# Moving forty matmuls behind the first output-projection rounds of every segment

## The chip, the cores and the metric

The kernel runs on one core of one Trainium2 chip. The metric is the device time of one launch in microseconds. Three runs of the kernel before took 1028.8, 1029.67 and 1029.64 us; their median is 1029.64 us.

## The reference

The input x has 2048 tokens of width 640. It is layer-normalised and goes through a recurrent attention of 64 segments of 32 tokens. Each segment attends to 8 memory rows and its own 32 tokens (causally), in 32 heads of width 128. The 8 output rows that belong to the memory are the memory of the next segment, so the segments form one serial chain. After that come a residual sum, a second layer norm, and a feed-forward block with a squared ReLU.

```python
for s in range(n_seg):                                   # 64 segments
    h = jnp.concatenate([mem, xs], axis=1)               # 8 memory rows + 32 tokens
    q = jnp.einsum('btd,dhe->bhte', h, Wq)               # k and v alike
    scores = jnp.where(mask, jnp.einsum('bhqe,bhke->bhqk', q, k) * scale, -1e9)
    o = jnp.einsum('bhqk,bhke->bhqe', _softmax(scores), v)
    o = jnp.einsum('bhte,hed->btd', o, Wo)
    mem = o[:, :M, :].copy()                             # feeds the next segment
    outs.append(o[:, M:, :])
# then h = x + attention, and h + (relu(norm(h) @ w1 + b1)**2) @ w2 + b2
```

## The kernel before, in words

All weights are held in SBUF as bf16, and the whole order of the work is written out by hand: each engine gets its instructions in the order of the Python text, and waits for others through semaphores.

`step(b, sp)` is one segment. Only the 8 memory rows depend on the segment before, and so the step takes them, with 24 of the tokens, through the projections; the last 8 tokens of four segments at a time ("tails") are projected ahead, as filler work (`fill`) in the later part of a step. `project` computes q and k in two halves each, with the small operand as the weights (`proj`, L206, 20 matmuls of 128x512 for a half, four column groups of TensorE at a time). Values go the same way: `ps0` is the even heads' half (20 matmuls), copied to `v[:, 0:512]` by ScalarE (L502), and `ps1` the odd heads' half, copied to `v[:, 512:1024]` (L523). "Even" and "odd" here are the heads whose index in the head group is in the first or second half of v; the code calls them n = 0 and n = 1.

Around the change TensorE's order in a step is this:

- two q and k projections with the scores of the memory rows of n = 0 between them;
- the first 8 matmuls of `ps0`, the token scores of n = 0 (`token_scores(0)`), the last 12 of `ps0`, the first 8 of `ps1`;
- the memory scores of n = 1 (`scores(1)`, L416 and L421, 20 matmuls), the token scores of n = 1 (L493, 16);
- `token_values` for the segment before (L355, 32 matmuls; L360, 8): probabilities of the previous step's tokens times the previous step's v, into columns 0 to 255 of the four banks of the PSUM tile `po`;
- `values(0)`: the memory rows' values of n = 0 (L449, 16 matmuls; L454, 4), into columns 256 to 287 of the same banks. They read `v[:, 0:512]` and the probabilities `pT0`, which VectorE has transposed (L440). VectorE copies the result to `oT` (L213, in `evac`);
- the last 12 matmuls of `ps1`;
- `wo_rounds(main, pw, 0, 6)`: 24 matmuls of the output projection (L238), whose weights are `oT`, n = 0;
- `values(1)` (L449, L454), which read `v[:, 512:1024]`; ScalarE copies their result (L215);
- `wo_rounds` 6 to 8 (8 matmuls), some filler, `wo_rounds` 8 to 16 (32), which need n = 1 of `oT`.

Then ScalarE and VectorE add the two halves of the output projection (`wo_out`, L245 and L246), ScalarE copies the token values out of `po` (`token_out`, L365), and `mem_to_hT` (L316, L318) puts the new memory rows in front of the next step's tokens. `po` has one buffer. Its first matmul into each bank of a step carries `start=True`, which opens the bank; all others add or write into what is opened.

Step 0 has no token values of a segment before; step 63 (`last`) has no memory values. After the steps the token values of segment 63 are made once more outside of `step` (L800), and then the feed-forward block runs in four tiles of 512 tokens.

Of the kernel before, what the change touches and what calls it, by code (L numbers as in the profile page):

```python
# [16 lines left out]
def kernel(  # L17
# [19 lines left out]
    M = A_mem0.shape[1]  # L37
# [8 lines left out]
    NS = S // SEG  # L46
# [48 lines left out]
    for g in range(G):  # L95
        r = slice(32 * g, 32 * g + 32)
# [15 lines left out]
    def head(p):  # L112

        n, g, j = p // 16, p // 4 % 4, p % 4
        return g * HG + j * 2 + n
# [115 lines left out]
    def wo_rounds(lhs, pw, h0, h1):  # L231

        for h in range(h0, h1):
            for kh in range(2):
                for ch in range(2):
                    j = kh * 2 + ch
                    p = h // 8 * 16 + kh * 8 + h % 8
                    nc.tensor.matmul(pw[32 * j:32 * j + 32, 0:DH], lhsT=lhs(p), rhs=wov2[:, head(p), ch],  # L238
                                     start=(h == 0), stop=(h == 15))
# [105 lines left out]
    oTg = oT[:].rearrange("p (n g j) q -> p n g j q", n=2, g=G)  # L345
    back = []

    def token_values(s, v, vt4, po):

        sp = s % 4  # L350
        pTk, pTx = back.pop()
        for i in range(HG):
            for g in range(G):
                r = slice(32 * g, 32 * g + 32)
                nc.tensor.matmul(po[:, g, i * 32:(i + 1) * 32], lhsT=v[r, i * E:(i + 1) * E], rhs=pTk[r, i, :],  # L355
                                 start=(i == 0), stop=False, skip_group_check=True)
        for u in range(2):
            for g in range(G):
                r = slice(32 * g, 32 * g + 32)
                nc.tensor.matmul(po[:, g, u * 128:(u + 1) * 128].rearrange("p (j q) -> p j q", q=32)[:, :, HD:32],  # L360
                                 lhsT=vt4[r, sp, u, :], rhs=pTx[r, u], start=False, stop=True, skip_group_check=True)

    def token_out(s, po):
        for n in range(2):
            nc.scalar.copy(out=oTg[:, n, :, :, M:NK],  # L365
                           in_=po[:, :, n * 128:(n + 1) * 128].rearrange("p g (j q) -> p g j q", q=32))
        nc.gpsimd.tensor_copy(out=oTts[s // 4 % 2][:, :, s % 4 * TL:(s % 4 + 1) * TL], in_=oT[:, :, 32:NK])
# [10 lines left out]
    prev = {}  # L378

    def step(b, sp, v=None):  # L380
        s = b * 4 + sp
        last = s == NS - 1
# [3 lines left out]
        if not ready:  # L386
            v = s2.tile([128, EG], BF16, tag="v", name="v")
# [55 lines left out]
        def values(n, pT, po):  # L443
            c0 = 256 + n * 4 * M
            for j in range(4):
                i = n * 4 + j
                for g in range(G):
                    r = slice(32 * g, 32 * g + 32)
                    nc.tensor.matmul(po[:, g, c0 + j * M:c0 + (j + 1) * M], lhsT=v[r, i * E:(i + 1) * E],  # L449
                                     rhs=pT[r, j * M:(j + 1) * M], start=(s == 0 and i == 0), stop=False,  # L450
                                     skip_group_check=True)
            for g in range(G):
                r = slice(32 * g, 32 * g + 32)
                nc.tensor.matmul(po[:, g, c0:c0 + 4 * M], lhsT=vt4[r, sp, n, :], rhs=pT[r, 32:64],  # L454
                                 start=False, stop=True, skip_group_check=True)

        def values_out(n, po):
            c0 = 256 + n * 4 * M
            evac(n == 0, oTg[:, n, :, :, 0:M], po[:, :, c0:c0 + 4 * M].rearrange("p g (j m) -> p g j m", m=M))
# [19 lines left out]
        vt4 = vt4s[b]  # L479
# [33 lines left out]
        if ready:  # L513
            run(fill, DC)
        po = pop.tile([128, G, 512], F32, tag="po", name="po")
        if s:
            token_values(s - 1, prev["v"], prev["vt4"], po)
        if not last:
            values(0, pT0, po)
            values_out(0, po)  # L520
# [10 lines left out]
        pw = chn.tile([128, 512], F32, tag="ch", name="pw")  # L531
        main = lambda p: oT[:, p, 0:32]
        wo_rounds(main, pw, 0, 6)
        if not last:
            values(1, pT1, po)
            values_out(1, po)
# [197 lines left out]
    for b in range(NB):  # L734
        for sp in range(4):
# [47 lines left out]
            if 2 <= e <= NK4 + 1:  # L783
                late.append(lambda e=e: prep_stats0(e - 2))
                mid.append(lambda e=e: prep_norm0(e - 2))
            step(b, sp, v0 if b + sp == 0 else None)

    def end_output(s):
# [8 lines left out]

    end_output(NS - 2)
    po = pop.tile([128, G, 512], F32, tag="po", name="po")
    token_values(NS - 1, prev["v"], prev["vt4"], po)  # L800
    token_out(NS - 1, po)
    for k in range(NK4):
        prep_bias(0, k, ht0[k][:])
# [3 lines left out]
    for t in range(S // NT):  # L807
# [6 lines left out]
        for fc in range(FC):  # L814
            ps = mmtile()
            for c in range(DC):
                if fc < FFULL:
                    nc.tensor.matmul(ps[:], lhsT=w1[:, c, fc * 128:(fc + 1) * 128], rhs=hnT[:, c, :],  # L818
                                     start=(c == 0), stop=(c == DC - 1))
                    continue  # L820
                for hh in range(2):
                    nc.tensor.matmul(ps[FREM * hh:FREM * (hh + 1), 0:HT], lhsT=w1[:, c, fc * 128:F],
                                     rhs=hnT[:, c, HT * hh:HT * (hh + 1)], start=(c == 0), stop=(c == DC - 1))
            w = NT if fc < FFULL else HT
            r = rs_[fc % 4]
# [14 lines left out]
        for q in range(NK4):  # L840
# [6 lines left out]
            for hh in range(2):  # L847
                k = pr + 2 * hh
                for fc in range(FFULL):
                    nc.tensor.matmul(y[:, hh, 0:DH], lhsT=f1T[:, fc, k * 128:(k + 1) * 128], rhs=w2[:, fc, cs],  # L850
                                     start=(fc == 0), stop=False, skip_group_check=True)
# [3 lines left out]
            for hh in range(2):  # L855
                r = slice(FREM * hh, FREM * (hh + 1))
                nc.tensor.matmul(y[:, hh, 0:DH], lhsT=f1T[r, FFULL, pr * 128:(pr + 1) * 128], rhs=w2[r, FFULL, cs],
                                 start=False, stop=True, skip_group_check=True)
# [40 lines left out]
```

## Time and profile before

| | |
|---|---|
| median of three runs | 1029.64 us |
| profiled execution, first to last instruction | 1025.5 us |
| what lies around it, to the median | 4.1 us |
| TensorE busy | 971.4 us, 95% |
| VectorE, ScalarE, GpSimd busy | 619.0, 533.2, 309.1 us |
| share of TensorE in the chain that ended last | 87% |
| granted TensorE clock, mean | 0.997 |
| first memory values to last token values | 53.5 to 890.1 us |
| token values, L355 and L360 | x2048 at 171 ns, x512 at 183 ns (median of one) |
| memory values, L449 and L454 | x2016 at 169 ns, x504 at 171 ns (median of one) |

The durations of single matmuls overlap: four or more run at a time in different parts of the array. What a group of matmuls costs is read from the starts: from the first start of a group to the first start of the next. In the step at 514 us, 32 token-value matmuls take 0.22 us in this way, though one is listed at 171 ns. "issue" in the answers is idle time for whose end the profile shows no other engine's work.

### The profile page before, as it was taken

What the parts mean: (1) busy time and instruction counts of PE and PEld (TensorE: products, weight loads), DVE (VectorE), ACT (ScalarE), POOL (GpSimd) and SP (SyncE); (2) the same over time, 40 slices, a digit from 0 to 9 for tenths busy, and PEclk for the clock granted to TensorE, in tenths of its full rate; (3) what the DMA queues carried; (4) which work ended last, traced back from release to release, by engine and by line L of the source; (5) the groups of instructions that cost most, each with busy time, mean ns of one, the idle gap of its engine ahead of it and who ended that gap; (6) DMA issues with size and microseconds to landing.
All of it is one profiled execution on the core that took longest, in us unless ns stands there. A gap on an engine that the chain in (4) does not pass through costs nothing.

```text
span 1025.5 us, 58960 instructions
## 1 busy us (share of the span) xinstructions
PE 971.4 (95%) x26951; PEld 576.6 (56%) x26960; DVE 619.0 (60%) x1740; ACT 533.2 (52%) x1229; POOL 309.1 (30%) x803
## 2 busy tenths in 40 slices
PE   5789999999999999999999999999999999999998
PEld 2345555655655555555655665555566565555565
DVE  2246666766666757666666666666666676466432
ACT  3335554555555555555555555555555555533431
POOL 1123333333333333333333332323232333443210
PEclk9989999999999999999999999999999999999999
DMA  9950101000101010001000000000000110612200
GB/s 367 397 180 21 23 7 30 7 25 6 35 7 31 6 40 8 26 11 31 11 25 11 26 16 20 17 15 27 14 22 8 47 34 7 204 55 65 77 26 26
DMA packets 39112, 51.57 MB, mean 50 GB/s; under 512 B 5968, under 2 KB 35024, under 8 KB 36944
## 3 DMA queue, kind: packets, MB, share of 16 engines
q1 hardware_dynamic: 38080, 47.48, 13.9%
q8 instruction: 210, 3.44, 1.4%
q10 hardware_dynamic: 784, 0.34, 0.1%
q14 instruction: 38, 0.31, 0.1%
HBM read 38.37 MB, written 9.44 MB: 47 GB/s over the span
## 4 chain that ended last, share of the span: by engine, by line
PE 87%; DMA 6%; DVE 2%; issue 2%; ACT 1%; SPq 1%; ACTq 0%; DVEq 0%; POOL 0%; POOLq 0%
PE ps L206 48%; PE pw L238 15%; PE y L850 5%; PE ps L818 4%; PE ps L238 3%; PE po L449 2%; PE po L355 2%; PE sm L421 2%; DMA wq<-in_B_w_dram 1%; DMA vt_d<-row 1%; PE ps L493 1%; DMA wv<-in_A_Wv_dram 1%; DMA wo<-in_A_Wo_dram 1%; PE pm L316 1%; DMA vt<-vt_d 1%
## 5 line engine op out<-in xcount | busy, mean ns | idle before, releaser
L206 PEld LDWEIGHTS <-hT 128*32 128x32 bf16 x7680 | 195.4, 97 | 179.6 <-issue 17.9
L238 PE MATMUL pw<-wo,oT 128*32 128x320 bf16 x4224 | 185.6, 300 | 7.6 <-issue 5.6
L206 PE MATMUL ps<-wv,hT 128*32 128x512 bf16 x2520 | 171.5, 379 | 2.3 <-issue 1.6
L206 PE MATMUL ps<-wq,hT 128*32 128x512 bf16 x2520 | 160.0, 382 | 5.3 <-DVE hT L318 5.3
L206 PE MATMUL ps<-wk,hT 128*32 128x512 bf16 x2520 | 159.3, 381 | 0.1
L238 PEld LDWEIGHTS <-oT 128*32 128x32 bf16 x4224 | 106.7, 96 | 59.8 <-issue 13.0
L222 ACT ACTIVATE row<-ps 128x512 bf16<-128x512 f32 x156 | 93.3, 599 | 75.5 <-PE ps L206 75.5
L227 DVE STREAM_TRANSPOSE qT<-row 128x512 bf16<-128x512 bf16 x128 | 90.3, 705 | 66.0 <-ACT row L222 65.9
L548 POOL TENSOR_TENSOR pkt<-ek,rk 128x64 bf16<-128x64 bf16 x64 | 18.8, 294 | 360.6 <-DVE rk L546 360.6
L224 ACT CAST row<-ps 128x512 bf16<-128x512 f32 x115 | 67.9, 591 | 33.1 <-PE ps L206 31.4
L325 POOL COPY kT<-kTt 128x1024 bf16<-128x1024 bf16 (+1 forms) x65 | 71.8, 1105 | 11.7 <-DVE kTt L227 11.7
L374 POOL COPY qz<-qT 128x96 bf16<-128x96 bf16 x126 | 33.4, 265 | 139.1 <-DVE qT L227 138.9
L206 PEld LDWEIGHTS <-hTt 128*32 128x32 bf16 x1920 | 53.6, 97 | 31.5 <-issue 1.3
L245 ACT COPY otmp<-pw 64x320 f32<-64x320 f32 x66 | 27.9, 422 | 81.3 <-PE pw L238 81.3
L365 ACT CAST oT<-po 128x512 bf16<-128x512 f32 x128 | 68.7, 589 | 1.6
L246 DVE TENSOR_TENSOR o<-pw,otmp 64x320 bf16<-64x320 f32 x66 | 31.8, 482 | 61.3 <-ACT otmp L245 61.3
L523 ACT CAST v<-ps 128x512 bf16<-128x512 f32 x63 | 36.9, 585 | 59.0 <-PE ps L206 59.0
L227 DVE STREAM_TRANSPOSE kT<-row 128x512 bf16<-128x512 bf16 x65 | 46.1, 709 | 31.1 <-ACT row L224 31.1
L544 DVE TENSOR_REDUCE zk<-ek 128x8 f32<-128x320 bf16 x64 | 31.1, 486 | 51.1 <-ACT ek L542 51.1
L850 PE MATMUL y<-wq,wk 128*128 128x320 bf16 x416 | 61.2, 299 | 0.4 <-DVE wk L827 0.4
L405 ACT CAST row<-ps 128x256 bf16<-128x256 f32 x126 | 40.7, 375 | 30.5 <-PE ps L206 29.9
L502 ACT CAST v<-ps 128x512 bf16<-128x512 f32 x63 | 36.9, 585 | 30.5 <-PE ps L206 30.5
(113 smaller groups left out, 1629.5 us busy)
## 6 DMA issues: line engine op xcount, KB each, us to landing
wv<-in_A_Wv_dram SPq DMA_DIRECT2D x5, 1024.0 KB
wq<-in_A_Wq_dram SPq DMA_DIRECT2D x5, 1024.0 KB
wk<-in_A_Wk_dram SPq DMA_DIRECT2D x5, 1024.0 KB
vt<-vt_d SPq DMA_DIRECT2D x60, 64.0 KB
xt<-in_A_x_dram SPq DMA_DIRECT2D x20, 160.0 KB
vt_d<-row SPq DMA_DIRECT2D x22, 128.0 KB
wo<-in_A_Wo_dram SPq DMA_DIRECT2D x2, 1280.0 KB
wo<-in_A_Wo_dram SPq DMA_DIRECT2D x4, 640.0 KB
```

What stands on the lines that cost most here:

```text
L206: nc.tensor.matmul(ps[32 * k:32 * k + 32, :], lhsT=lhs(c), rhs=wr[:, c, n, k], start=(c == 0), stop=(c == DC - 1))
L222: nc.scalar.mul(out=row, in_=ps, mul=scale)
L224: nc.scalar.copy(out=row, in_=ps)
L227: nc.vector.transpose(out=dst[:, n * 16:(n + 1) * 16, 0:32], in_=row.rearrange("p (h e) -> p h e", e=32))
L238: nc.tensor.matmul(pw[32 * j:32 * j + 32, 0:DH], lhsT=lhs(p), rhs=wov2[:, head(p), ch], start=(h == 0), stop=(h == 15))
L325: nc.gpsimd.tensor_copy(out=kT[:, h0:h1, SEG:2 * SEG].rearrange("p h (j k) -> p h j k", k=TL), in_=k.unsqueeze(2).to_broadcast([128, h1 - ...
L365: nc.scalar.copy(out=oTg[:, n, :, :, M:NK], in_=po[:, :, n * 128:(n + 1) * 128].rearrange("p g (j q) -> p g j q", q=32))
L405: nc.scalar.copy(out=row[:, u * 256:(u + 1) * 256], in_=ps[:, u * 256:(u + 1) * 256])
L502: nc.scalar.copy(out=v[:, 0:512], in_=ps0[:])
L523: nc.scalar.copy(out=v[:, 512:1024], in_=ps1[:])
L818: nc.tensor.matmul(ps[:], lhsT=w1[:, c, fc * 128:(fc + 1) * 128], rhs=hnT[:, c, :], start=(c == 0), stop=(c == DC - 1))
L850: nc.tensor.matmul(y[:, hh, 0:DH], lhsT=f1T[:, fc, k * 128:(k + 1) * 128], rhs=w2[:, fc, cs], start=(fc == 0), stop=False, skip_group_chec ...
```

## The change

The call of `token_values` for the segment before moves: from ahead of `values(0)` to behind the first 24 output-projection matmuls, ahead of `values(1)`. Which matmul opens the banks changes with it: `values(0)` does in every step that has memory values, and `token_values` only in the last step and in the call after the steps. Nothing else is edited.

```diff
-    def token_values(s, v, vt4, po):
+    def token_values(s, v, vt4, po, opens):
...
                 nc.tensor.matmul(po[:, g, i * 32:(i + 1) * 32], lhsT=v[r, i * E:(i + 1) * E], rhs=pTk[r, i, :],
-                                 start=(i == 0), stop=False, skip_group_check=True)
+                                 start=(opens and i == 0), stop=False, skip_group_check=True)
...
-                                     rhs=pT[r, j * M:(j + 1) * M], start=(s == 0 and i == 0), stop=False,
+                                     rhs=pT[r, j * M:(j + 1) * M], start=(i == 0), stop=False,
...
         po = pop.tile([128, G, 512], F32, tag="po", name="po")
-        if s:
-            token_values(s - 1, prev["v"], prev["vt4"], po)
         if not last:
             values(0, pT0, po)
             values_out(0, po)
...
         wo_rounds(main, pw, 0, 6)
+        if s:
+            token_values(s - 1, prev["v"], prev["vt4"], po, last)
         if not last:
             values(1, pT1, po)
             values_out(1, po)
...
-    token_values(NS - 1, prev["v"], prev["vt4"], po)
+    token_values(NS - 1, prev["v"], prev["vt4"], po, True)
```

## The prediction

> **What bounds the kernel now.** I read the page first, then TensorE's waits, then single steps in the timeline.
>
> ```profile
> span 1025.5 us, 58960 instructions
> ...
> PE 971.4 (95%) x26951; PEld 576.6 (56%) x26960; DVE 619.0 (60%) x1740; ACT 533.2 (52%) x1229; POOL 309.1 (30%) x803
> ...
> q8 instruction: 210, 3.44, 1.4%
> ...
> PE 87%; DMA 6%; DVE 2%; issue 2%; ACT 1%; SPq 1%; ACTq 0%; DVEq 0%; POOL 0%; POOLq 0%
> ```
>
> TensorE is the chain, so a change counts by what it does to TensorE's idle time. Queue 8 brings instructions: 210 packets, 3.44 MB, 16 KB each. TensorE has 53,911 records, so a packet holds 256 instructions, or 128 matmuls with their weight loads: call it a block.
>
> ```profile
> PE pw L238 <- issue: 5.6, 14, 1.2
> ...
> PE po L449 <- issue: 4.4, 10, 0.7
> ...
> PE po L454 <- issue: 1.8, 4, 0.6
> ...
> PE ps L206 <- issue: 1.6, 4, 0.6
> ```
>
> This is TensorE idle with nobody to wait for, 13 us in 32 places. One of them, in the step at 252 us:
>
> ```profile
> 252.65 0.37 PE L355 MATMUL po<-pTk,v 32*128 32x32 bf16 x32
> ...
> 252.93 0.17 PE L449 MATMUL po<-pTm,v 32*128 32x8 bf16 x1
> ...
> 253.81 0.26 PE L449 MATMUL po<-pTm,v 32*128 32x8 bf16 x15 [0.70 <-issue]
> ```
>
> The second memory-value matmul comes 0.88 us after the first, in the middle of a group that runs at 7 ns a matmul elsewhere. I numbered all matmuls in program order and compared each one's distance from its predecessor with the median of the same place in other steps. 55 of those up to 890 us are late, **27.6 us together**, and all of them have a number that leaves 93 on division by 128. They are block edges; 53 lie at the places below, the other two (2.2 us) outside of steps 1 to 62. After a late edge the next packet begins 1.13 us later (median; 1.05 to 1.29 for most), a packet takes 1.07 us on average, and TensorE goes on 1.41 us after its end: **3.6 us from asking to having**. A block that is run in less makes TensorE wait. [...]
>
> An undisturbed step:
>
> ```profile
> 514.16 0.58 ACT L502 CAST v<-ps 128x512 bf16<-128x512 f32 x1 [0.48 <-PE ps L206]
> ...
> 514.74 0.37 PE L355 MATMUL po<-pTk,v 32*128 32x32 bf16 x32
> ...
> 515.03 0.30 PE L449 MATMUL po<-pTm,v 32*128 32x8 bf16 x16
> ...
> 515.29 0.83 PE L206 MATMUL ps<-wv,hT 128*32 128x512 bf16 x12
> ...
> 515.95 0.99 PE L238 MATMUL pw<-wo,oT 128*32 128x320 bf16 x24
> 516.15 0.24 DVE L440 STREAM_TRANSPOSE pTm<-pmem 128x64 bf16<-128x64 bf16 x1
> 516.18 0.58 ACT L523 CAST v<-ps 128x512 bf16<-128x512 f32 x1 [0.75 <-PE ps L206]
> ...
> 516.87 0.17 PEld L449 LDWEIGHTS <-v 32*128 32x128 bf16 x16 [0.27 <-ACT v L523]
> ```
>
> By starts: token values 0.284 us (medians of 62 steps here and below), memory values 0.268, end of `ps1` 0.658, 24 output-projection matmuls 0.921. The copy of even values (L502) ends as the token values start: these now cover it.
>
> **The change part by part.** Counted in matmuls from the first token value of before, the four groups stand at 0-39, 40-59, 60-71 and 72-95; after, memory values at 0-19, `ps1` at 20-31, output projection at 32-55, token values at 56-95. The matmuls are as many, so every block edge keeps its number.
>
> *Term 1, the wait for even values.* `values(0)` now follows the token scores at once and must wait for L502, which ends 7 ns after its new place (5 to 7 in 61 of the 62 steps 1 to 62). From a ScalarE copy's end to the matmul that waits for it takes 50 to 52 ns where TensorE was idle (L502 to L206 at 868.84 us). So 57 to 59 ns a step; 62 x 0.058 = **+3.6 us**. The upper bound is the only longer distance from copy to matmul here, 111 ns from L523 to the second memory values: 62 x 0.118 = 7.3 us. I take the lower, because 111 is no wait: the start after the last output-projection matmul is 232 ns there, as at L180 with nothing to wait for. `pT0` (L440) is done 0.23 us before, 0.07 in the worst step. Behind the waiting weight load stand 20 memory values, `ps1` and 24 output-projection matmuls; L213 and L523 wait for those, and both come 0.23 us earlier than now, since the token values no longer stand ahead. `oT` reaches the output projection 0.12 us early in either order.
>
> *Term 2, odd values.* `values(1)` gets 0.284 us more cover after L523, but it doesn't wait now (232 ns as above): 0. The token values need what the last step left, long done. Changes between kinds of groups are as many as before. Step 63 and the call after the steps have no memory values and get no new wait. ScalarE's and GpSimd's steps after the output projection keep their distance to it, and no DMA moves: 0.
>
> *Term 3, edges at 32 to 95.* The block's predecessor edge lies 128 matmuls earlier, ahead of the moved groups, so the packet comes when it came; TensorE now reaches the edge later, because slow groups (`ps1`, output projection) stand ahead of it in place of the quick token values. Later by 0.97 us at 40, 1.49 at 56, 1.39 at 60, 1.00 at 71, 0.59 at 80 and 0.06 at 96 (sums of the groups above). 26 of the 55 waits lie here, 14.8 us. Less the shift of its own place each, 0.5 us is left: **-14.3 us**.
>
> *Term 4, edges at 96 to 127.* 15 waits, 6.0 us; each edge is reached 0.058 us later, packet as before: **-0.9 us**.
>
> *Term 5, edges at 128 to 159.* Their predecessors lie at 0 to 31. 37 edges, 12 waits, 4.6 us. [...] Lowest: only the 0.058 us shift counts, -0.6. Highest: all 37 wait 0.3 us more, +11. I take 0.25 us, the middle of 0.2 and 0.3, at the 12 that wait, **+3.0**, and nothing for the 25 that are on time, whose slack the trace does not tell; this is the term that I know least.
>
> Sum: 3.6 - 14.3 - 0.9 + 3.0 = -8.6. On the profiled execution 1025.5 becomes 1016.9; the 4.1 us around it stay: **1021.0 us**.
>
> [...]
>
> **The rivals.**
>
> *Slower: the waits move, they don't go.* A block edge's wait that is avoided could return at the next edge, because TensorE arrives there sooner after the request. For it: an edge at 56 was passed at 0.42 us plus its wait of some 0.6, now at 1.90, so the way to the next is up to 1.4 us shorter. Against: the next edge, at 160 to 223, lies in filler and projections at 54 ns a matmul, and no edge there waits in the trace. If all comes back, term 1 decides: 1029.64 + 3.6 = 1033.2. It is slower once less than 3.6 us of the 27.6 goes. [...]
>
> *Half:* term 5 at its upper bound, 3.6 - 14.3 - 0.9 + 11 = -0.6: 1029.0, no change.
>
> *More:* term 5 at its lower bound: 3.6 - 14.3 - 0.9 - 0.6 = -12.2: 1017.4.
>
> *Term 1 at its upper bound* with the rest as forecast: -4.9, 1024.7.
>
> **How the numbers follow.** Forecast 0.56 (within 1018 to 1024), more 0.10, term 1 larger 0.16, half 0.06, slower 0.12. No change is within 0.2%, 2.06 us, about what a measurement of this kernel can tell. Faster: the first three, 0.82; same 0.06; slower 0.12. The range leaves out the slower rival and half of "half" at the top and the end of "more" at the bottom: 1016.5 to 1028.0.
>
> **What would show it.** Term 1: the first memory-value matmul about 50 ns after L502's end in every step, with the wait listed. Terms 3 to 5: late edges at 32 to 95 gone, about 13 us of 27.6 gone in all, and the "issue" lines at L449 and L454 smaller; those at L238 8 to 16 stay. Wrong if late edges appear in places from 160 on, if the copy-to-matmul distance is over 0.1 us, or if packets start later than before for edges whose predecessor is ahead of the moved groups.

## The result and the profile after

The changed kernel took 1019.41 us (median of four runs, 1016.66 to 1022.05) against 1029.66 us before. The ratio is 0.9899, with a 95% interval of 0.9877 to 0.9922: about 10.4 us faster. A second measurement gave 1018.82 us, ratio 0.9897 (0.9878 to 0.9915).

The following lines of the changed kernel's page answer to those shown of the kernel before. Its profiled execution took 1020.98 us; the span from the first to the last instruction is 2.2 us shorter.

```profile
span 1018.8 us, 58958 instructions
...
PE 972.1 (95%) x26951; PEld 582.4 (57%) x26960; DVE 621.6 (61%) x1740; ACT 533.8 (52%) x1229; POOL 309.3 (30%) x803
...
q8 instruction: 210, 3.44, 1.4%
...
PE 88%; DMA 6%; DVE 2%; issue 1%; ACT 1%; SPq 0%; DVEq 0%; POOL 0%; ACTq 0%; POOLq 0%
```

TensorE works as long as before (972.1 against 971.4 us), and as many packets of instructions are fetched. What went is idle time without a releaser, "issue" in the chain: 2% before, 1% now. TensorE's waits, changed kernel (total us, times, longest us):

```profile
PE pw L238 <- issue: 5.4, 15, 1.2
...
PE po L449 <- issue: 1.4, 4, 0.5
...
PE po L454 <- issue: 0.4, 1, 0.4
```

At the memory values it fell from 4.4 + 1.8 us to 1.4 + 0.4, and the 1.6 us at L206 are no longer listed; at the output projection it stayed (5.6 to 5.4). An undisturbed step of the changed kernel in the timeline (start us, us, engine, line, operation; L521 is L523 of before):

```profile
512.19 0.59 ACT L502 CAST v<-ps 128x512 bf16<-128x512 f32 x1 [0.48 <-PE ps L206]
...
512.83 0.26 PE L449 MATMUL po<-pTm,v 32*128 32x8 bf16 x16
...
513.06 0.83 PE L206 MATMUL ps<-wv,hT 128*32 128x512 bf16 x12
...
513.72 0.99 PE L238 MATMUL pw<-wo,oT 128*32 128x320 bf16 x24
513.94 0.59 ACT L521 CAST v<-ps 128x512 bf16<-128x512 f32 x1 [0.48 <-PE ps L206]
...
514.64 0.37 PE L355 MATMUL po<-pTk,v 32*128 32x32 bf16 x32
...
514.92 0.29 PE L449 MATMUL po<-pTm,v 32*128 32x8 bf16 x16
```

L502 ends at 512.78 and the even heads' memory values start at 512.83. Over the 62 steps with a projection of values this distance has a median of 55 ns; before, it was 278 ns. In 60 of the 62 it is 54 or 55 ns, so TensorE now waits for the copy in nearly every step. The list of idle times has no line for that wait, since the matmuls ahead are still listed as running: the last group of token scores goes from 512.55 to 512.83 there. Such ends are modelled, not measured.

The step at 252 us, whose second memory-value matmul came 0.88 us after the first, in the changed kernel:

```profile
251.72 0.26 PE L449 MATMUL po<-pTm,v 32*128 32x8 bf16 x16
251.83 0.18 PE L454 MATMUL po<-pTm,vt 32*128 32x32 bf16 x4
251.94 0.83 PE L206 MATMUL ps<-wv,hT 128*32 128x512 bf16 x12
```

The group runs through. Its block edge has the same number, but that number now belongs to the output projection.

**The account.** In all traces below, matmuls are numbered in program order and each start is compared with the median distance for its place. "Late edges" is the sum over matmuls whose number leaves 93 on division by 128 and that are more than 40 ns late; "the rest" is the time of the 62 steps less that sum. The stretch is 62 steps, from the token scores of segment 1 to those of segment 63.

| kernel (one profiled execution each) | 62 steps, us | late edges, us (how many of 194) | the rest, us |
|---|---|---|---|
| before | 811.5 | 25.5 (54) | 786.0 |
| changed | 806.0 | 14.7 (38) | 791.3 |
| changed, measured again | 801.6 | 10.6 (38) | 791.0 |
| before, 24 matmuls more at the start | 816.0 | 28.6 (55) | 787.4 |
| changed, 80 matmuls more at the start (195 edges) | 805.9 | 13.6 (38) | 792.3 |
| tail matmuls ahead of the even memory values | 805.5 | 19.4 (57) | 786.2 |
| token values right behind the even memory values | 830.2 | 4.6 (17) | 825.6 |
| token values behind the last round | 799.2 | 2.4 (13) | 796.8 |
| tail matmuls ahead, the others behind the last round | 795.7 | 2.6 (18) | 793.1 |

The change costs 5 us in the rest and takes 11 to 15 us of late edges away. Between the profiles themselves the 62 steps are 5.5 and 9.9 us shorter, where the medians of the runs differ by 10.2 and 10.5. By place, counted as in the prediction, the late edges are, in us:

| place | edges | before | changed | changed, measured again |
|---|---|---|---|---|
| 32 to 95 | 30 | 14.8 | 0.3 | 0.4 |
| 96 to 127 | 15 | 6.0 | 6.9 | 5.0 |
| 128 to 159 | 17 | 4.6 | 5.5 | 4.0 |
| 160 and on | 115 | 0.1 | 2.0 | 1.2 |

### The profile page after: what moved, and what is told of

The parts are those of the page before. It is cut to its first block, busy times and chain, and to the rows that moved or that the text cites. A ratio compares the mean times of both kernels' runs of the same rounds, so it can differ in the third digit from the quotient of the medians.

```text
span 1018.8 us, 58958 instructions
## 1 busy us (share of the span) xinstructions
PE 972.1 (95%) x26951; PEld 582.4 (57%) x26960; DVE 621.6 (61%) x1740; ACT 533.8 (52%) x1229; POOL 309.3 (30%) x803
## 4 chain that ended last, share of the span: by engine, by line
PE 88%; DMA 6%; DVE 2%; issue 1%; ACT 1%; SPq 0%; DVEq 0%; POOL 0%; ACTq 0%; POOLq 0%
PE ps L206 48%; PE pw L238 15%; PE y L850 6%; PE ps L818 5%; PE ps L238 3%; DMA wk<-in_A_Wk_dram 3%; PE po L449 2%; PE po L355 2%; PE sm L421 2%; DMA wq<-in_B_w_dram 1%; DMA xt<-in_A_x_dram 1%; PE ps L493 1%; PE pm L316 1%; PE ps L489 1%; DVE o L246 1%
## 5 line engine op out<-in xcount | busy, mean ns | idle before, releaser
L206 PEld LDWEIGHTS <-hT 128*32 128x32 bf16 x7680 | 200.9, 97 | 171.6 <-issue 14.2
L206 PE MATMUL ps<-wv,hT 128*32 128x512 bf16 x2520 | 170.5, 379 | 0.9 <-ACT v L502 0.7
L206 PE MATMUL ps<-wq,hT 128*32 128x512 bf16 x2520 | 160.2, 381 | 5.3 <-DVE hT L318 5.3
L206 PE MATMUL ps<-wk,hT 128*32 128x512 bf16 x2520 | 159.5, 380 | 0.1
L238 PEld LDWEIGHTS <-oT 128*32 128x32 bf16 x4224 | 104.6, 96 | 60.5 <-ACT oT L215 13.6
L206 PEld LDWEIGHTS <-hTt 128*32 128x32 bf16 x1920 | 55.0, 97 | 32.3 <-issue 3.7
L521 ACT CAST v<-ps 128x512 bf16<-128x512 f32 x63 | 36.9, 586 | 30.7 <-PE ps L206 30.7
L502 ACT CAST v<-ps 128x512 bf16<-128x512 f32 x63 | 36.9, 586 | 30.0 <-PE ps L206 30.0
```

Source lines behind the costliest of these rows:

```text
L206: nc.tensor.matmul(ps[32 * k:32 * k + 32, :], lhsT=lhs(c), rhs=wr[:, c, n, k], start=(c == 0), stop=(c == DC - 1))
L502: nc.scalar.copy(out=v[:, 0:512], in_=ps0[:])
```

## The experiments

The theories. A: the gain is block edges that TensorE no longer reaches ahead of their packet, because slow groups stand ahead of the token values; the wait for L502 is its price. B: the gain comes from the even heads' memory values, and all that follows from them on VectorE, coming earlier. C: the gain is the token values' cover for the copy of the odd values.

### A block edge by itself

```diff
+            if (b, sp) == (8, 0):
+                pad = pop.tile([128, G, 512], F32, tag="po", name="pad")
+                for i in range(256):
+                    for g in range(G):
+                        r = slice(32 * g, 32 * g + 32)
+                        nc.tensor.matmul(pad[:, g, i % 8 * 32:i % 8 * 32 + 32], lhsT=ident[r, :], rhs=ident[r, 0:32],
+                                         start=True, stop=True)
             step(b, sp, v0 if b + sp == 0 else None)
```

> The kernel before, with 1024 extra matmuls of the token values' kind (32 rows by 128 columns of weights, 32 columns moved, four row groups), without any wait, ahead of segment 32; their result is not used. Measures a block edge by itself. Theory A: 128 matmuls cannot pass in less than the 3.6 us that lie between asking for a packet and having it, so each of the 8 edges in them is late, by about 2.7 us (3.6 less 0.9 of running), and the 1024 take about 26 to 29 us in place of 1024 x 7 ns = 7.2 us. Any theory without edges: about 7.2 us, and no gap in them.

1059.76 us in its one run, 30.5 us above the median of the kernel before measured with it. The 1024 matmuls start between 470.0 and 498.1 us, so they take 28.1 us. TensorE's timeline of this kernel (the bracket is the idle time ahead):

```profile
470.05 0.95 PE L791 MATMUL pad<-ident 32*128 32x32 bf16 x99
472.51 1.19 PE L791 MATMUL pad<-ident 32*128 32x32 bf16 x128 [1.52 <-issue]
476.26 1.23 PE L791 MATMUL pad<-ident 32*128 32x32 bf16 x128 [2.56 <-issue]
479.73 1.22 PE L791 MATMUL pad<-ident 32*128 32x32 bf16 x128 [2.25 <-issue]
483.20 1.22 PE L791 MATMUL pad<-ident 32*128 32x32 bf16 x128 [2.25 <-issue]
487.22 1.22 PE L791 MATMUL pad<-ident 32*128 32x32 bf16 x128 [2.80 <-issue]
...
```

There are no waits on other engines in these 1024, and TensorE stops after every 128. The DMA records show what it stops for: one 16 KB packet of queue 8 begins 1.07 to 1.56 us after each edge, and TensorE goes on 1.18 to 1.59 us after that packet's end. From one edge to the next it is 3.47, 3.75 or 4.02 us, and never less; the matmuls themselves start 8 ns apart. That is the 3.6 us of the prediction, measured without anything else. The mechanism of A is there, and B and C have no place for these gaps; how much of the gain it makes is what the table and the other runs tell.

### The same work with other numbers

Before, with 24 matmuls on the identity in the first microseconds, and the changed kernel with 80 of them:

```diff
+    pad = mm.tile([128, 512], F32, tag="mm", name="pad")
+    for _ in range(24):
+        nc.tensor.matmul(pad[:, 0:128], lhsT=ident[:], rhs=ident[:], start=True, stop=True)
     ln_stats(0)
```

> The kernel before, with 24 extra matmuls on TensorE in the first microseconds, while it waits for the first normalised tokens; all later work is the same in the same order, with its number 24 higher. Theory A: every late matmul has a number that leaves 93 on division by 128 again, so the late ones are other matmuls than before, 24 places earlier in the order; the sum of lateness changes to about 22 us from 27.6, time about 1025.5 us. A theory in which the late matmuls are late for the work they stand in (a bank, a port, a semaphore): the same matmuls are late and the time is 1029.6 us or a little more.

1029.68 us, ratio 0.9989 (0.9975 to 1.0002): no clear difference. The late matmuls still leave 93 on division by 128, so they are other matmuls than before: not one of the late ones is the same, though all work after the first microseconds is. No remainder but 93 has more than 3.2 us of lateness in either profile (from 60 to 890 us). So in these two profiles the number decides which matmul is late, and the work around it only whether an edge costs anything: at places 32 to 95, 26 of 30 edges are late before and 23 of 27 after the shift, and from 160 on 1 of 115 and 4 of 113. The sum and the time were misses: 28.6 us, not 22, and no gain of 4 us. The time alone is what a theory without edges had said; the numbers of the late matmuls are what speaks for A.

> The changed kernel with 80 extra matmuls in the first microseconds, which move every block edge 80 places earlier in the later work. Theory A: the edges fall on other places; by the positions, about 3 us less lateness than the changed kernel, 1016 to 1019 us. Theories that leave the edges out: the time of the changed kernel, or a little more.

1020.61 us, ratio 0.9917 (0.9895 to 0.9939), beside 0.9897 (0.9878 to 0.9915) of the changed kernel measured with it. No gain: a miss, and by time alone this too is what theories without edges had said. Late edges are 13.6 us, between the two executions of the changed kernel; at 128 to 159 they fell to 3.0 us, from 160 on they rose to 3.6. So the edges did not become cheaper by this shift, and the run decides nothing between the theories. Which numbers the edges get moves the time of either kernel by no more than I can tell; the order of the groups moves it by 10 us.

> The changed kernel once more, beside the others of this call on one chip: 1019 to 1022 us, 0.988 to 0.992 of the kernel before. To be compared with the next two.

1018.82 us, just under the expected 1019 to 1022, and a ratio within the expected one. Its profile shows how far one execution differs from the next: 10.6 us of late edges, not 14.7, and 1017.61 us for the execution, not 1020.98. The rest is the same to 0.3 us. So the scatter between those two executions lies in the late edges.

### The wait for the even values

In the changed kernel, the 8 tail matmuls of the token values go back ahead of the even heads' memory values and open the banks:

```diff
+    def tail_values(s, vt4, po):
...
+                                 lhsT=vt4[r, sp, u, :], rhs=pTx[r, u], start=(u == 0), stop=False, skip_group_check=True)
...
         po = pop.tile([128, G, 512], F32, tag="po", name="po")
+        if s:
+            tail_values(s - 1, prev["vt4"], po)
         if not last:
             values(0, pT0, po)
...
         wo_rounds(main, pw, 0, 6)
         if s:
-            token_values(s - 1, prev["v"], prev["vt4"], po, last)
+            token_values(s - 1, prev["v"], po)
```

> The changed kernel, but the 8 tail matmuls (L360) stand ahead of the even heads' memory values again and open the banks; the 32 others stay behind the output projection's first rounds. Tells what the wait for L502 costs. If term 1 is right (57 to 62 ns a step at 62 steps), 8 matmuls of 0.07 us cover the wait: 3.5 to 4.5 us faster than the changed kernel, about 1015.5 us, with about as much in late edges (16 to 17 us). If the wait were hidden anyway, no faster than the changed kernel; 8 more quick matmuls ahead of the edges at 40 to 95 would then cost up to 1 us.

1018.15 us, ratio 0.9866 (0.9844 to 0.9888), some 0.3 percentage points under the changed kernel, with intervals that overlap. The expected gain of 3.5 to 4.5 us over the changed kernel is thus not shown in the time, and 1015.5 us was a miss. The account is clearer: the rest is 786.2 us, that of before, against 791.0 and 791.3. The 8 matmuls take 64 ns by starts, and the token scores ahead of them go on after 230 ns as before, against 293 in the changed kernel. So the wait is real and costs what the rest shows, 4.8 to 5.1 us. The late edges rose, to 19.4 us in its profiled execution (1021.32 us, the slowest of its six) where 16 to 17 were expected, and that takes the gain back: edges at 32 to 95 cost 2.5 us again, those from 160 on 3.6.

The same run speaks against B: the even memory values start 0.22 us earlier here than before, and the rest is no shorter.

### Token values right behind the even memory values

```diff
             values_out(0, po)
+        if s:
+            token_values(s - 1, prev["v"], prev["vt4"], po, last)
...
         wo_rounds(main, pw, 0, 6)
-        if s:
-            token_values(s - 1, prev["v"], prev["vt4"], po, last)
```

> The token values stand right behind the even heads' memory values, ahead of the end of ps1 and of the output projection. So the even values' copy is waited for as in the changed kernel, and the even heads' memory values leave TensorE as early; but the token values are among quick groups again. Theory A (the gain is late block edges that vanish because slow groups stand ahead of the token values): late edges are back, about 26 us of them, and the wait for L502 stays, so about 1033 us, 3 to 4 us slower than before. Theory B (the gain comes from the even memory values, their copy L213 and the second softmax running 0.23 us earlier): as fast as the changed kernel, 1019 to 1020 us.

1045.94 us, ratio 1.0137 (1.0114 to 1.0159): slower than either theory said. The waits and the timeline of this kernel tell why:

```profile
PE po L355 <- DVE oT L213: 26.2, 62, 0.5
```

```profile
524.70 0.18 PE L454 MATMUL po<-pTm,vt 32*128 32x32 bf16 x4
...
524.96 0.29 DVE L213 CAST oT<-po 128x128 bf16<-128x128 f32 x1 [0.19 <-PE po L454]
...
525.30 0.37 PE L355 MATMUL po<-pTk,v 32*128 32x32 bf16 x32 [0.42 <-DVE oT L213]
```

The token values write `po` while VectorE reads other columns of it, and the program gives them a wait for that read. By starts, the last four memory-value matmuls go on after 0.60 us here; in the changed kernel the next group comes after 0.11. In the changed kernel the 24 output-projection matmuls ahead of them need L213's result as weights, and its list of waits has no line at L355. With that wait in every step (0.42 us, 26.2 us in 62), late edges fall to 4.6 us. So the run doesn't decide between A and B as I had meant it to. It shows that edges cost little (17 of 194 late, 4.6 us) in a kernel where TensorE waits for something else in every step, and that the place behind the output projection's first rounds has a second merit that I had not seen.

### Token values behind the last round

```diff
         wo_rounds(main, pw, 0, 6)
-        if s:
-            token_values(s - 1, prev["v"], prev["vt4"], po, last)
...
         wo_rounds(main, pw, 8, 16)
+        if s:
+            token_values(s - 1, prev["v"], prev["vt4"], po, last)
```

> The token values stand behind the last output-projection round (rounds 8 to 16), no longer between rounds 6 and the odd heads' memory values. Theory A (block edges): hardly any quick stretch is long enough to outrun a packet, 1 to 5 us of late edges are left instead of 16.8 us, but two more changes between kinds of groups cost some 0.11 us a step (about 7 us): 1014 to 1018 us. Theory C (the gain is the token values' cover for the copy of the odd values, L523 of before): that cover is gone as it was before, and the even values' copy is waited for, so 1033 us or more.

1014.11 us, ratio 0.9835 (0.9812 to 0.9859), as theory A said. Late edges fall to 2.4 us, and the rest rises to 796.8, 5.5 to 5.8 above the changed kernel: the token values stand alone now, between groups of another shape, and by group medians the last round goes on after 1.19 us instead of 1.10, the tail matmuls after 0.17 instead of 0.07. C falls: the odd values have no cover here, as before, and the kernel is faster still. The one line of idle time without releaser that is left in TensorE's waits:

```profile
PE pw L238 <- issue: 2.1, 2, 1.4
```

### Both findings together

The tail matmuls ahead of the even memory values, the 32 others behind the last round:

```diff
         wo_rounds(main, pw, 0, 6)
-        if s:
-            token_values(s - 1, prev["v"], po)
...
         wo_rounds(main, pw, 8, 16)
+        if s:
+            token_values(s - 1, prev["v"], po)
```

> Both findings together: the 8 tail matmuls stand ahead of the even heads' memory values (no wait for L502), the 32 other token-value matmuls behind the last output-projection round. Theory A: late edges as few as there (5 us or less), and the 0.06 us a step of the wait for L502 is saved: 4 us faster than with all token values behind the last round, about 1010 us, 0.979 to 0.981 of the kernel before.

1009.13 us, ratio 0.9804 (0.9784 to 0.9825), as expected: 20 us faster than before, and faster than the changed kernel, whose interval beside it (0.9878 to 0.9915) lies wholly above. The page and TensorE's waits of this kernel:

```profile
span 1007.5 us, 59032 instructions
...
PE 91%; DMA 5%; DVE 3%; issue 1%; ACT 1%; SPq 0%; DVEq 0%; POOL 0%; ACTq 0%; POOLq 0%
```

```profile
PE pw L238 <- issue: 1.9, 2, 1.3
```

TensorE's share of the chain rose from 87% to 91%. Late edges are 2.6 us, the rest is 3.7 us under that of the run before: the wait for L502, once more.

## Why the prediction was right, point by point

The time, 1021.0 us, lies inside the measured runs, 1.6 us above the median. The cause is the one predicted: late edges at 32 to 95 go, and a wait for L502 is the price. That the sum comes so close is in part luck, since term 5 was too large while the price in the rest and the edges from 160 on were set too low.

*Term 1, +3.6 us:* right in kind, somewhat too small. The copy-to-matmul distance is 55 ns, not 111. By group medians the token scores last 62.5 ns longer, the even memory values 44 less, the odd ones 41 more: 60 ns net, 3.7 us in 62 steps. The rest rose by 5.0 to 5.3 us. Of the other 1.3 to 1.6, some 0.7 us lie behind the odd memory values, up to the memory rows' way into the next step: the last round of the output projection, which needs L215's copy of them, now starts 52 ns after that copy's end (median; 89 before), as after a wait. The prediction had put nothing there. What is left is not traced.

*Term 2, 0:* the odd values had no wait to lose, as said. That the token values behind the 24 output-projection matmuls meet no wait was right, but I didn't name the one that they would have had a place earlier, L213.

*Term 3, -14.3 us:* right, -14.4 and -14.5 in the two profiles. This is more than the whole net gain.

*Term 4, -0.9 us:* not decided. +0.9 in one execution and -1.0 in the other: 15 edges whose packets come when they come.

*Term 5, +3.0 us:* too large; +0.9 and -0.6 measured. No run shows the 0.2 to 0.3 us a wait that it is added up from: the packets that follow the edges at places 0 to 31 begin 1.09 us after place 0 before and 1.05 after the change (medians of 17), so all that moved is place 0 itself, by 0.06 us. The prediction's 37 edges at 128 to 159 was a miscount, which had taken in places up to 199; there are 17. Its upper bound of +11 was therefore too high by more than half: the 17 at 0.3 us give 5. The rival "half" had no ground.

*The slower rival* was partly there: waits did return at later edges, where none had been, but 2.0 and 1.2 us of the 14.4, not all. The prediction held that no edge from 160 on waits (the trace before has one, of 0.1 us); 11 and 7 do. Its own sign for a fault ("late edges in places from 160 on") was thus met, at a cost that the oversized term 5 happened to cover.

Against the execution of before, the two of the changed kernel show in the 62 steps: the rest +5.3 and +5.0, late edges -10.8 and -14.9, so -5.5 and -9.9 us. The first of the two is one of the slower executions. What lies around the span is 2.1 to 2.2 us wherever a run lists both, so the 4.1 us that the prediction added to the profiled execution of before was partly the distance of that execution from the median.

## What to carry to other kernels

Idle time of TensorE without a releaser is worth locating by instruction number. Here it recurred at a fixed remainder, 93 on division by 128, beside the instruction packets of queue 8, and what took 11 to 15 us of it away was slow matmuls ahead of the quick ones; the least that passed from edge to edge in the stretch of 1024 was 3.47 us. Moving the quick work had a price of its own: the copy that it covered (0.06 to 0.08 us a step) and, in one place, a read of a PSUM tile that it had to wait for (0.42 us a step). Eight of the quick matmuls left in front (64 ns) covered the one, and a place behind a group that needs the result of that read anyway avoided the other. Such a gain shows up only in sums over many steps: of some 194 edges in 62 steps 54 were late before, and the table by place shows them spread over the step.

## What the runs showed of the hardware

In the stretch of 1024 quick matmuls the distance from edge to edge was 3.47 us four times, 3.745 twice and 4.02 once, 0.274 us apart; I don't know why. Nor did TensorE wait after every block that was run in less than the prediction's 3.6 us: in the 62 steps 53 of 77 such edges were late before, and 34 of 102 in the changed kernel (the distance from the edge before, less the lateness itself). And two executions of the changed kernel differ by 4 us in late edges alone (14.7 and 10.6), so here a difference of less than that between the times of two profiles is no finding; the rest agreed to 0.3 us between them.
